# Row statistics of a tuned FNet/H3 kernel: eight rows' scaling, epsilon and bias moved from VectorE into ScalarE passes

## The chip, the core and the metric

The kernel runs on one core of a Trainium2 chip. A core has five engines, each with a queue of its own that it works off in order: TensorE (in the profile PE for matrix products and PEld for the loading of their weights), VectorE (DVE), ScalarE (ACT), GpSimd (POOL) and SyncE (SP), which here only issues transfers. An engine waits for another by a semaphore that stands on an instruction, and all that stands behind a waiting instruction waits with it. The metric is the device time of one execution in microseconds (us). Before the change it is 1183.71 us, the median of three runs (1183.38 to 1183.75).

## The reference, cut to what matters

```python
x = x + A(layernorm(x))      # layer 1
x = x + B(layernorm(x))      # layer 2
x = x + A(layernorm(x))      # layer 3
x = x + B(layernorm(x))      # layer 4

def layernorm(x):            # over the 576 channels of a row, eps = 1e-5
    return (x - mean(x)) / sqrt(var(x) + eps)

def A(x):                    # Fourier mixing, dft matrices given as arrays
    a = x @ dft_hid_re.T;  b = x @ dft_hid_im.T
    return dft_seq_re @ a - dft_seq_im @ b

def B(x):                    # gate: x times a long causal convolution
    kv = short_conv(k, shift_k) * v          # does not depend on x
    return x * (long_conv_fft(kv, ssm_k) + kv * ssm_D)
```

`x` is 2048 rows of 576 channels in float32. Only the normalisation of layer 1's input is touched by the change.

## The kernel before, in words

The 2048 sequence rows are cut into sixteen "rows" of 128 partitions by 576 channels; the text below calls them row 0 to row 15. Layer 1 multiplies them with the sequence matrix first. `layer` walks through 4 column blocks (`tb`) times 2 matrices (`g`, real and imaginary) times 16 rows (`k`), 128 steps in all. A step takes one 128x512 piece of the matrix (`c_mat`, loaded by SP, line 169) and one row of x. To keep float32 accuracy from products of a shorter float type, both are split into a high and a low part: ScalarE copies the high part (line 99 for the matrix, line 197 for a row of x), VectorE subtracts it from the source and keeps the low part (line 100 for the matrix, lines 204 and 205 for x). A step is 14 matmuls of 128x512: three (high by high, high by low, low by high) for each of four accumulators `s0` to `s3` and two for the remainder `rm`. The split pieces of the matrix lie in a ring of three, so a new one is written when the products of three steps before it are over.

The rows of x are needed one after the other in the first sixteen steps (`g` = 0, `tb` = 0). `get_x` is called three steps ahead (`XLEAD`): it asks for the row's load, takes its statistics (`stats0`) and normalises it in place, and `to_x` makes the two parts. Rows 0 to 7 have their statistics from VectorE (`normed`: bn_stats, bn_aggr, line 183 on). Rows 8 to 15 (`ASTAT` = 8) use `normed_x` with `sums`: ScalarE runs over the row with an accumulated sum (line 656), VectorE scales it to minus the mean (line 657), ScalarE runs again with that mean as bias, squares and accumulates (line 658), VectorE scales the sum and adds epsilon (line 659), GpSimd raises it to the power -0.5 (line 660), VectorE multiplies mean and factor to a bias (line 693), and ScalarE normalises (line 694). The three VectorE pieces are 128x1. Layers 2 to 4 use `sums` and `normed_x` too.

Beside these steps runs `branch`, the part of B that does not depend on x. In this stretch it makes the short convolution on VectorE (line 399 products, line 404 sums, both 128x1152; line 432 times v) and its first Fourier stage on TensorE: groups of six matmuls into the banks `bf` (`f1_products`), evicted by ScalarE into a staging tile `so` (line 458), which a transfer on ScalarE's queue stores to DRAM (line 459). There are four staging tiles, so an eviction waits until the store of four groups before it has landed. GpSimd's queue also loads the stage's matrices (line 173).

The program is written as one stream, and a scheduler with an own idea of the costs puts the instructions of each engine in an order; `behind` (`issue_after`) sets a few orders by hand. That order is fixed when the kernel runs.

## Time and profile before

| | before |
|---|---|
| median of three runs | 1183.71 us |
| the profiled execution: its time | 1181.68 us |
| its span, first to last instruction | 1179.9 us |
| TensorE busy | 1167.4 us, 99% of the span |
| VectorE busy | 869.3 us, 74% |
| ScalarE busy | 650.1 us, 55% |
| GpSimd busy | 76.3 us, 6% |

The profile is of one execution. Its page gives busy times by engine, and its views answer from the same trace: a timeline in order of time, groups of equal instructions, who waited for whom, and busy times in chosen windows. In a timeline row stand the start (us from the span's start), the duration, the engine, the source line, the operation, what it writes and reads, and how many equal ones follow each other; a bracket says how long the engine was idle before it and what ended that. The rows with "ACTq" or "SPq" are transfers being issued from an engine's queue. Matmuls overlap in the pipeline, so a run of twelve is read by the start of what follows it, not by the sum of the durations. Busy shares of the whole span are averages; the change touches only some 40 us of them near the start.

### The profile page before, as it was taken

Reading aid. Unit: us, or ns where it says so; the run is one execution under the profiler, and the core shown is the slowest. Engines: PE = TensorE matmul, PEld = TensorE weight load, DVE = VectorE, ACT = ScalarE, POOL = GpSimd, SP = SyncE. Lnnn points to the kernel's source line nnn. Section 1 sums busy time; section 2 is a strip of 40 time slices with the busy share of each in tenths; the row PEclk is TensorE's granted clock in tenths of the full one; section 3 lists DMA queues with packets and bytes.
Section 4 is the critical chain, followed back from the end, with each engine's and each line's share of the span. In section 5 each row is a group of like instructions: output and inputs, shape, how many; then the busy total and the mean of one; then the engine's idle time right before and its main releaser. Section 6 shows DMA issues by size and latency. Waiting matters only on the chain.

```text
span 1179.9 us, 18085 instructions
## 1 busy us (share of the span) xinstructions
PE 1167.4 (99%) x6198; PEld 988.8 (84%) x6198; DVE 869.3 (74%) x1564; ACT 650.1 (55%) x1280; POOL 76.3 (6%) x115
## 2 busy tenths in 40 slices
PE   8999999999999999999999999999999999999997
PEld 6776667988888888898888898888888888889997
DVE  7899983788877778777757765865776776775764
ACT  7865655577766667766645666534434445450200
POOL 2310000000000000001101111000000000001111
PEclk9999999999999999999999999999999999999999
DMA  9879898545666656648966777762862787895621
GB/s 337 284 230 308 267 293 289 164 151 171 211 215 196 203 168 202 182 149 245 269 187 221 244 251 226 256 237 76 257 247 72 223 291 251 262 329 152 222 89 41
DMA packets 147453, 255.64 MB, mean 217 GB/s; under 512 B 16161, under 2 KB 56353, under 8 KB 147362
## 3 DMA queue, kind: packets, MB, share of 16 engines
q1 hardware_dynamic: 111890, 210.17, 55.5%
q10 hardware_dynamic: 28560, 37.91, 9.1%
q0 software_dynamic: 6912, 6.43, 2.5%
q8 instruction: 48, 0.79, 0.3%
q14 instruction: 43, 0.35, 0.1%
HBM read 187.80 MB, written 66.65 MB: 216 GB/s over the span
## 4 chain that ended last, share of the span: by engine, by line
PE 86%; DVE 5%; DMA 4%; ACT 3%; issue 1%; SPq 0%; ACTq 0%; DVEq 0%
PE s L76 49%; PE bk L76 29%; PE rm L76 5%; PE bf L76 2%; DMA yb<-flts 2%; DMA flts<-in_c_mat 1%; ACT flts L519 1%; DVE f1f L404 1%; DVE f1f L399 1%; ACT mid L519 1%; DVE mats L100 1%; ACT mats L99 0%; DVE mid L525 0%; DVE f1r L100 0%; DMA ph<-in_c_mat 0%
## 5 line engine op out<-in xcount | busy, mean ns | idle before, releaser
L76 PE MATMUL s<-mats 128*128 128x512 f32 x2102 | 546.3, 395 | 4.2 <-DVE mats L766 1.5
L76 PEld LDWEIGHTS s<-mats 128*128 128x128 f32 x2102 | 382.4, 188 | 87.1 <-issue 10.8
L100 DVE TENSOR_TENSOR mats<-flts,mats 128x512 fp32r<-128x512 f32 x206 | 140.9, 688 | 51.6 <-ACT mats L99 49.7
L99 ACT ACTIVATE mats<-flts 128x512 fp32r<-128x512 f32 x206 | 128.2, 627 | 80.6 <-PE bk L76 31.1
L76 PE MATMUL bk<-mid 128*128 128x288 f32 x704 | 126.3, 300 | 0.8 <-ACT flts L519 0.2
L519 ACT ACTIVATE flts<-bk 128x288 f32<-128x288 f32 (+1 forms) x192 | 76.7, 406 | 90.8 <-PE bk L76 74.0
L76 PEld LDWEIGHTS bk<-mid 128*128 128x128 f32 x704 | 108.6, 188 | 21.2 <-ACT flts L519 4.8
L76 PE MATMUL bk<-w,u 128*128 128x288 f32 x864 | 120.3, 295 | 0.0
L76 PEld LDWEIGHTS bk<-w,u 128*128 128x128 f32 x864 | 117.4, 188 | 2.9 <-ACT flts L519 0.9
L525 DVE TENSOR_TENSOR mid<-flts,mid 128x576 fp32r<-128x576 f32 (+1 forms) x149 | 93.4, 627 | 18.9 <-ACT mid L519 16.0
L76 PE MATMUL rm<-mats 128*128 128x512 f32 x304 | 94.5, 390 | 0.2 <-ACT flts L519 0.2
L519 ACT ACTIVATE mid<-flts 128x576 fp32r<-128x576 f32 (+1 forms) x148 | 80.6, 576 | 9.1 <-DVE flts L540 5.1
L293 DVE TENSOR_TENSOR flts<-flts,bk 128x288 f32<-128x288 f32 x48 | 21.8, 454 | 68.6 <-PE bk L76 68.5
L76 PE MATMUL bk<-mats 128*128 128x288 f32 (+1 forms) x376 | 67.8, 317 | 0.0
L76 PEld LDWEIGHTS rm<-mats 128*128 128x128 f32 x304 | 56.9, 188 | 12.7 <-ACT flts L519 0.6
L458 ACT ACTIVATE flts<-bf 128x384 f32<-128x384 f32 (+1 forms) x104 | 43.3, 461 | 42.1 <-PE bf L76 39.8
L76 PE MATMUL s<-t,mats 128*128 128x512 f32 x264 | 64.9, 389 | 0.0
L186 POOL TENSOR_TENSOR flts<-flts 128x1 f32<-128x1 f32 x34 | 28.6, 843 | 515.6 <-DVE flts L185 514.1
L76 PE MATMUL bk<-mats,t 128*128 128x288 f32 (+1 forms) x368 | 59.3, 303 | 0.0
L519 ACT ACTIVATE flts<-flts 64x288 f32<-64x288 f32 x128 | 56.6, 443 | 4.5
L76 PEld LDWEIGHTS bk<-mats 128*128 128x128 f32 x376 | 55.6, 188 | 3.4
L76 PEld LDWEIGHTS s<-t,mats 128*128 128x128 f32 x264 | 49.5, 188 | 10.3
(152 smaller groups left out, 1495.9 us busy)
## 6 DMA issues: line engine op xcount, KB each, us to landing
flts<-in_c_mat SPq DMA_DIRECT2D x148, 256.0 KB, 3.5
ph<-in_c_mat SPq DMA_DIRECT2D x54, 512.0 KB, 4.2
flts<-in_c_mat SPq DMA_DIRECT2D x30, 512.0 KB, 5.2
flts<-td SPq DMA_DIRECT2D x53, 288.0 KB, 3.0
td<-flts ACTq DMA_DIRECT2D x36, 384.0 KB, 4.2
vd<-flts ACTq DMA_DIRECT2D x64, 144.0 KB, 2.4
flts<-vd SPq DMA_DIRECT2D x32, 288.0 KB, 4.1
ud<-ph ACTq DMA_DIRECT2D x12, 512.0 KB, 6.4
```

The lines of the kernel that those rows point to most:

```text
L76: return nc.tensor.matmul(ps, lhsT, rhs, start=first, stop=last, skip_group_check=more).ins
L99: a = nc.scalar.activation(h, src, AF.Copy).ins
L100: return a, nc.vector.tensor_tensor(l, src, h.bitcast(F32), OP.subtract).ins
L186: pows.append(nc.gpsimd.tensor_tensor(rs, ve, mhalf, OP.pow).ins)
L293: added[:] = [nc.vector.tensor_tensor(r[:, cs], r[:, cs], ps[:, :HD], OP.add).ins]
L399: nc.vector.tensor_tensor(out_t[:, n], k, wt[3 - t][:, n], OP.mult)
L404: nc.vector.tensor_tensor(rp, rp, out_t, OP.add)
L458: stored[:] = [nc.scalar.activation(so[:, i, :], ps[i], AF.Copy).ins]
L519: last_act.append(nc.scalar.activation(*args, **kw).ins)
L525: nc.vector.tensor_tensor(l, src, h.bitcast(F32), OP.subtract)
```

## The change

A new function `normed_first` serves rows 8 to 15 of layer 1 in place of `normed_x`. The scale by -1/576 goes into the first pass of ScalarE, so that its accumulated sum is minus the mean at once. The scale of the squares and the epsilon become a ScalarE instruction of 128x1 (Identity with scale 1/576 and bias epsilon), and the bias, mean times factor, becomes another one (Copy with the factor as scale). GpSimd's power stays. So for each row three VectorE instructions of 128x1 go and two ScalarE instructions of 128x1 come. `sums` and `normed_x` stay as they are for the later layers.

```diff
+    def normed_first(src, y, junk):
+        m = ring["stat"]()
+        sm, sv, rs, nb = (m[:, i:i + 1] for i in range(4))
+        nc.scalar.activation(junk, src, AF.Copy, scale=-1.0 / D, accum_out=sm)
+        nc.scalar.activation(junk, src, AF.Square, bias=sm, accum_out=sv)
+        nc.scalar.activation(sv, sv, AF.Identity, bias=eps, scale=1.0 / D)
+        pows.append(nc.gpsimd.tensor_tensor(rs, sv, mhalf, OP.pow).ins)
+        yield
+        nc.scalar.activation(nb, sm, AF.Copy, scale=rs)
+        nc.scalar.activation(y, src, AF.Identity, bias=nb, scale=rs)
+
 ...
-            LN[j] = src, normed_x(src, src, ring["junk"]()) if j >= ASTAT else normed(src, src)
+            LN[j] = src, normed_first(src, src, ring["junk"]()) if j >= ASTAT else normed(src, src)
```

In the changed file the new lines are 699 (sum), 700 (squares), 701 (epsilon), 702 (power), 704 (bias) and 705 (normalise); lines from 707 on are 11 higher than before. The scheduler has made another order of it. It differs from the old one from the statistics of row 8 on until the first Fourier stage has done its first twenty groups or so, about the first 150 us; behind that only buffer numbers differ.

First place: ScalarE, where rows 11 to 13 are handled. Before, with what each instruction waits for in brackets (the engines' semaphores; DMAHW is a transfer):

```order
L694 ACTIVATE early<-early,flts 128x576 [waits DVE_49]
L99 ACTIVATE f1r<-f1f 128x576 [waits DVE_49]
L197 ACTIVATE mats<-early 128x576 [waits Activation_49]
L99 ACTIVATE mats<-flts 128x512 [waits DMAHW4_49,PE_49]
L656 ACTIVATE early,flts<-early 128x576 [waits DMAHW0_49]
L459 DMA td<-flts 256x1x288
L459 DMA td<-flts 256x1x288 [waits DMAHW5_49]
L658 ACTIVATE early,flts<-early,flts 128x576 [waits DVE_49]
L694 ACTIVATE early<-early,flts 128x576 [waits DVE_49]
L658 ACTIVATE early,flts<-early,flts 128x576 [waits DVE_49]
L197 ACTIVATE mats<-early 128x576 [waits Activation_49]
```

The same place of ScalarE's queue in the change, from row 11's high part to row 12's:

```order
L197 ACTIVATE mats<-early 128x576 [waits Activation_49]
L99 ACTIVATE f1r<-f1f 128x576 [waits DVE_49]
L458 ACTIVATE flts<-bf_66 128x288 [waits DMAHW7_49,PE_49]
L458 ACTIVATE flts<-bf_67 128x288
L99 ACTIVATE mats<-flts 128x512 [waits DMAHW1_49]
L699 ACTIVATE early,flts<-early 128x576 [waits DMAHW6_49]
L704 ACTIVATE flts<-flts 128x1 [waits Pool_49]
L700 ACTIVATE early,flts<-early,flts 128x576 [waits Activation_49]
L705 ACTIVATE early<-early,flts 128x576 [waits Activation_49]
L701 ACTIVATE flts<-flts 128x1 [waits Activation_49]
L197 ACTIVATE mats<-early 128x576 [waits Activation_49]
```

No pass of the statistics waits for VectorE any more. Two rows are interleaved, so that hardly an instruction needs the one directly ahead of it, and what waits for GpSimd is now ScalarE (L704).

Second place: VectorE in the same stretch, where the low part of step 11's matrix piece (`mats<-flts,mats`) is made. Before:

```order
L432 TENSOR_TENSOR f1f<-f1f,flts 128x576 [waits DMAHW6_49,DVE_49]
L399 TENSOR_TENSOR f1f<-f1f 128x1152
L659 TENSOR_SCALAR flts<-flts 128x1 [waits Activation_49]
L399 TENSOR_TENSOR f1f<-f1f 128x1152
L204 TENSOR_TENSOR mats<-early,mats 128x64 [waits Activation_49]
L205 TENSOR_TENSOR mats<-early,mats 128x512
L100 TENSOR_TENSOR f1r<-f1f,f1r 128x576 [waits DVE_49]
L100 TENSOR_TENSOR mats<-flts,mats 128x512 [waits DMAHW2_49,PE_49]
L657 TENSOR_SCALAR flts<-flts 128x1
L693 TENSOR_TENSOR flts<-flts 128x1 [waits Pool_49]
L100 TENSOR_TENSOR mats<-flts,mats 128x512 [waits DMAHW4_49,PE_49,Activation_49]
```

In the change, the same piece of work:

```order
L404 TENSOR_TENSOR f1f<-f1f 128x1152 [waits DVE_49]
L100 TENSOR_TENSOR mats<-flts,mats 128x512 [waits DMAHW3_49,PE_49,Activation_49]
L432 TENSOR_TENSOR f1f<-f1f,flts 128x576 [waits DMAHW5_49,DVE_49]
L399 TENSOR_TENSOR f1f<-f1f 128x1152 x2
L204 TENSOR_TENSOR mats<-early,mats 128x64 [waits Activation_49]
L205 TENSOR_TENSOR mats<-early,mats 128x512
L100 TENSOR_TENSOR f1r<-f1f,f1r 128x576 [waits Activation_49]
L100 TENSOR_TENSOR mats<-flts,mats 128x512 [waits DMAHW1_49,PE_49,Activation_49]
```

The 128x1 instructions and their waits for GpSimd are gone, and the two-input instructions stand directly behind each other.

Third place: ScalarE near the last rows, with a store (L459) and the eviction that waits for its landing through the same staging tile (L458 with the same DMAHW name). Before:

```order
L459 DMA td<-flts 256x1x288 [waits DMAHW2_49]
L694 ACTIVATE early<-early,flts 128x576 [waits DVE_49,Activation_49]
L99 ACTIVATE f1r<-f1f 128x576
L197 ACTIVATE mats<-early 128x576 [waits Activation_49]
L458 ACTIVATE flts<-bf_66 128x288 [waits DMAHW5_49,PE_49]
L458 ACTIVATE flts<-bf_67 128x288
```

In the change:

```order
L459 DMA td<-flts 256x1x288 [waits DMAHW4_49]
L704 ACTIVATE flts<-flts 128x1 [waits Pool_49]
L700 ACTIVATE early,flts<-early,flts 128x576 [waits Activation_49]
L705 ACTIVATE early<-early,flts 128x576 [waits Activation_49]
L701 ACTIVATE flts<-flts 128x1 [waits Activation_49]
L197 ACTIVATE mats<-early 128x576 [waits Activation_49]
L458 ACTIVATE flts<-bf_68 128x288 [waits DMAHW4_49,PE_49]
```

Before, the DMAHW5 of the eviction was the store that stood some twenty-five instructions ahead; in the change the store that the eviction waits for stands five computing instructions ahead of it. On SP's queue one load of x has moved ahead of one load of the matrix at about 5.6 us.

## The prediction, as it was put on record

> **What bounds the kernel now.** I read the page first, then the windows of the first 140 us, TensorE's timeline there for its gaps, and at each gap the timeline of the engine that ended it. The page says who is the bound:
>
> ```profile
> PE 1167.4 (99%) x6198; PEld 988.8 (84%) x6198; DVE 869.3 (74%) x1564; ACT 650.1 (55%) x1280; POOL 76.3 (6%) x115
> ```
>
> TensorE is busy for all but 12.5 us of the 1179.9 us span, and the change takes no matmul away. Only gaps of TensorE can be won, and only where the new order differs, in the first 150 us or so. The windows where rows 8 to 15 are made, and one behind them (x is a count; the values are busy us of 10):
>
> ```profile
> 40.00:50.00 10.00, 10.00 (x51) 7.64 (x49) 9.62 (x16) 8.85 (x21) 5.80 (x2) 1.00 0.95 324
> 50.00:60.00 10.00, 9.16 (x42) 6.28 (x40) 7.93 (x20) 8.16 (x17) 1.10 (x2) 1.00 0.42 148
> 60.00:70.00 10.00, 10.00 (x51) 7.69 (x49) 9.56 (x17) 7.47 (x16) 2.05 (x3) 1.00 0.75 225
> 110.00:120.00 10.00, 10.00 (x50) 7.07 (x50) 10.00 (x12) 5.95 (x13) 0.53 (x1) 1.00 0.99 329
> ```
>
> The columns are TensorE, its weight loads, VectorE, ScalarE, GpSimd, the granted clock (1.00), and transfers. TensorE loses time in 50 to 60 us (9.16, 42 matmuls instead of 51). TensorE's timeline shows where, and one later gap:
>
> ```profile
> 42.87 3.05 PE L76 MATMUL s<-mats 128*128 128x512 f32 x12
> 45.75 0.62 PE L76 MATMUL rm<-mats 128*128 128x512 f32 x2
> ...
> 50.06 0.96 PE L76 MATMUL s<-mats 128*128 128x512 f32 x3
> 51.62 2.35 PE L76 MATMUL s<-mats 128*128 128x512 f32 x9 [0.60 <-DVE mats L100]
> 53.81 0.62 PE L76 MATMUL rm<-mats 128*128 128x512 f32 x2
> 54.67 1.91 PE L76 MATMUL s<-mats 128*128 128x512 f32 x6 [0.25 <-ACT mats L197]
> ...
> 119.04 1.66 PE L76 MATMUL s<-mats 128*128 128x512 f32 x6
> 121.03 0.79 PE L76 MATMUL bf<-f1r 64*128 64x384 f32 x6 [0.32 <-ACT flts L458]
> ```
>
> The ends of matmuls are modelled, so I price a gap by starts. Undisturbed, twelve matmuls behind a bf group take 45.75 - 42.87 = 2.88 us, 0.24 each. Step 11 starts at 50.06; its fourth matmul was due at 50.78 and comes at 51.62: 0.84 lost to a low part that VectorE made late. The two remainder matmuls at 53.81 need about 0.48, so step 12 was due at 54.29 and starts at 54.67: 0.38 lost to row 12's high part on ScalarE. Together 1.2 us. At 119.04 six matmuls need 1.44 and the group comes at 121.03: some 0.5 lost, while VectorE is 100% busy.
>
> Why both parts were late stands in ScalarE's timeline:
>
> ```profile
> 24.92 0.67 ACT L656 ACTIVATE early<-early 128x576 f32<-128x576 f32 x1
> ...
> 35.82 0.78 ACT L658 ACTIVATE early<-early,flts 128x576 f32<-128x576 f32 x1 [0.38 <-DVE flts L657]
> 36.50 0.19 ACT L658 ACTIVATION_READ_ACCUMULATOR early<-early,flts 128x1 f32 x1
> 36.59 0.85 ACT L694 ACTIVATE early<-early,flts 128x576 f32<-128x576 f32 x1
> 37.35 0.61 ACT L99 ACTIVATE mats<-flts 128x512 fp32r<-128x512 f32 x1
> ...
> 40.18 0.52 ACTq L459 DMA_DIRECT2D td<-flts  x1
> ...
> 40.66 0.68 ACT L197 ACTIVATE mats<-early 128x576 fp32r<-128x576 f32 x1
> 41.23 0.69 ACT L458 ACTIVATE flts<-bf 128x288 f32<-128x288 f32 x2
> 41.81 0.62 ACT L99 ACTIVATE mats<-flts 128x512 fp32r<-128x512 f32 x1
> ...
> 51.66 0.78 ACT L658 ACTIVATE early<-early,flts 128x576 f32<-128x576 f32 x1 [1.92 <-DVE flts L657]
> ...
> 53.95 0.67 ACT L197 ACTIVATE mats<-early 128x576 fp32r<-128x576 f32 x1
> ```
>
> ScalarE stood 1.92 us just before the second gap, for a 0.15 us VectorE instruction that was queued behind convolution work. The view of waits adds such pieces up for the first 100 us:
>
> ```profile
> DVE flts L693 <- POOL flts L660: 3.8, 7, 0.7
> ACT early L658 <- DVE flts L657: 3.8, 6, 1.9
> ...
> ACT early L694 <- DVE flts L693: 1.3, 2, 0.7
> ...
> DVE flts L659 <- ACT early L658: 0.9, 3, 0.5
> ```
>
> **The change part by part.** *Taken from VectorE:* eight each of L657, L659 and L693. They show 0.15 us but follow each other closer than that:
>
> ```profile
> 38.12 0.15 DVE L659 TENSOR_SCALAR flts<-flts 128x1 f32<-128x1 f32 x1
> 38.18 0.14 DVE L657 TENSOR_SCALAR flts<-flts 128x1 f32<-128x1 f32 x1
> ```
>
> So 24 x 0.06 to 0.07 = 1.6 us of queue, and the waits of 3.8 and 0.9 with them: 6.3 us that VectorE's queue gains over some 38 us, far over the 0.84 by which step 11's low part was late. This gap goes unless ScalarE is late.
>
> *Added to ScalarE:* two instructions of 128x1 for each of eight rows. Before has no such pair; the nearest are these:
>
> ```profile
> 2.04 0.20 ACT L177 ACTIVATE flts<-flts 128x1 f32<-128x1 f32 x1
> 1174.54 0.29 ACT L672 ACTIVATE flts<-flts 128x1 f32<-128x1 f32 x1 [50.95 <-DVE flts L670]
> ```
>
> 16 x 0.20 = 3.2 us to 16 x 0.29 = 4.6 us. I take 0.20, since neighbours overlap by 0.1 (L694 shows 0.85 and its successor starts 0.76 later), but keep 0.29. Against it stand the waits of 3.8 + 1.3 = 5.1 us that end. Whether row 12 is in time I add up along the new order, from the first pass of row 8 (24.92 before, and the queue ahead of it is unchanged) to row 12's L197. Start to start a squares pass with its read of the accumulator takes 0.77 (35.82 to 36.59), a normalising pass 0.76, L197 0.57 (40.66 to 41.23), an eviction 0.29 (two to 41.81); a matrix split is 0.62 less the overlap of 0.1, and a sum pass with its read 0.67 + 0.19 less twice 0.1. There stand 6 sum passes (4.0), 6 squares (4.6), 6 normalisings (4.6), 6 L197 (3.4), 8 evictions (2.3), 5 splits (2.6), one f1r copy (0.6) and 11 small ones (2.2 to 3.2): 24.3 to 25.3 us. L197 of row 12 would start at 49.2 to 50.2 instead of 53.95. It is due, with 0.84 no longer lost, at about 53.4: a lead of 3.2 to 4.2 us, and step 12's 0.38 goes too. The same sum to row 15 gives a lead of 2.5 to 3.3.
>
> *The new wait:* L704 on ScalarE waits for GpSimd's power, and behind it stand the next row's squares and a matrix split. The new order leaves 1.1 to 3.1 us of other passes, mostly 2.4, between L701 that starts a power and its L704. The power takes 0.55 when undisturbed, which that covers; the worst row is dearer:
>
> ```profile
> 41.88 4.20 POOL L660 TENSOR_TENSOR flts<-flts 128x1 f32<-128x1 f32 x1 [2.99 <-DVE flts L659]
> 52.79 0.55 POOL L660 TENSOR_TENSOR flts<-flts 128x1 f32<-128x1 f32 x1 [2.83 <-DVE flts L659]
> ```
>
> VectorE says why:
>
> ```profile
> 41.85 1.35 DVE L399 TENSOR_TENSOR f1f<-f1f 128x1152 f32<-128x1152 f32 x1
> 43.12 0.69 DVE L205 TENSOR_TENSOR mats<-early,mats 128x512 fp32r<-128x512 f32 x1
> 43.72 1.35 DVE L404 TENSOR_TENSOR f1f<-f1f 128x1152 f32<-128x1152 f32 x1
> 44.99 0.69 DVE L100 TENSOR_TENSOR mats<-flts,mats 128x512 fp32r<-128x512 f32 x1
> 45.59 0.15 DVE L657 TENSOR_SCALAR flts<-flts 128x1 f32<-128x1 f32 x1
> ```
>
> That power ended at 46.08, 0.4 after the last of four two-input instructions (44.99 + 0.69 = 45.68): it got in when the one-input L657 came. Until now one in eight was caught so long. One caught power costs ScalarE 4.2 - 2.4 = 1.8 us, within the lead; an undisturbed one nothing. I take one such row, so nothing on the path. The Trainium skill, "SBUF — State Buffer", "Who interferes with whom", says that a VectorE instruction with two SBUF inputs holds the port pair shared with GpSimd for the whole instruction, and that whoever starts first blocks the other. Its tie of the blocking to two inputs agrees with the rows; but read as first come, first served, a power would wait for one instruction alone, 1.35 + 0.4 = 1.8 us at most, under most of the cover of 2.4, and the slower rival below would have no chance. The row at 41.88 lost three handovers instead, so the measurement decides, and that rival keeps its chance.
>
> *Stores moved:* L459 now stands five computing instructions ahead of an eviction that waits for its landing, some 2.1 us. The view of that line, 20 to 75 us:
>
> ```profile
> DMA to landing us min/median/max: 2.9/4.1/8.1
> ```
>
> ScalarE's queue issues a store a few places early (at 40.18, before L197 and two evictions that stand ahead of it had started), some 2 us more. So a store costs nothing at the median and 4 us at 8.1, which the lead all but covers; I take nothing. SP's swap puts one matrix piece one issue later; its split is not the next thing ScalarE does, so nothing. GpSimd's own loads (L173) stand behind the powers in the same order as before, and wait for TensorE.
>
> *Later:* behind the rows VectorE is the tight queue (10.00 of 10 in the window of 110 to 120) and has the same work as before. With its 6.3 us it should start on it early enough not to take back TensorE's 1.2; of the 0.5 at 121.03 I count nothing, its other end being all of it.
>
> Sum: 0.84 + 0.38 = 1.2 us less, the other terms zero. The profiled execution (1181.68, the span and 1.8 around it) lies 2.03 under the median; taken off the median, 1183.71 - 1.2 = 1182.5.
>
> **The rivals.** *The gain is used up* (0.20): one or two powers or stores are caught late in the row sequence, where the lead is shortest (2.5), and TensorE waits about as long as it did: 1183.4 to 1184.3.
>
> *ScalarE becomes the bound* (0.26, slower): VectorE no longer pauses, so powers stay locked out; its only one-input instructions there are the ones removed. Each costs 1.8 us as above. With the lead of 3.5 plus the 1.2 won, it decides from the third caught row on; four caught rows give 7.2 - 3.5 = 3.7 lost against 1.2 before, 1183.7 + 2.5 = 1186.2. For it speaks that VectorE's new order has runs of six or more two-input instructions; against it, that VectorE waits for ScalarE's L197 in each row, and there GpSimd gets in.
>
> *The later gap goes as well* (part of the forecast's range): 1.2 + 0.5, 1182.0. That the change does not do what it says cannot be: the new order has no 128x1 VectorE instruction for these rows.
>
> **How the numbers follow.** The forecast, 1181.6 to 1183.3, has 0.50; a gain beyond it, from an order that fits better for a reason I don't see, 0.04. The low end is 1183.71 - 1.7 - 0.4 for what three runs vary (1183.38 to 1183.75); the high end, 1186.0, leaves out about half of the slower rival. 0.2% is 2.4 us, about what can be told from no change here; faster than 1181.3 gets 0.04, slower than 1186.1 0.13, and the rest, 0.83, lies within.
>
> **What would show it.** Right: no gap at steps 11 and 12; L197 of row 12 starting near 50; no waits of ScalarE on VectorE for statistics; L704 waiting under 2 us in all. Wrong: powers of 3 us and more in a row with ScalarE idle "<-POOL", evictions waiting for "DMA td" or a gap of TensorE behind L99 or L197 in steps 13 to 16.

## The result: the gaps of steps 11 and 12 are gone, and the kernel is 0.9 to 1.8 us slower

| | before | changed | ratio, 95% interval |
|---|---|---|---|
| first comparison, median of 22 runs each | 1183.5 us | 1185.32 us | 1.0016 [1.0010, 1.0022] |
| second, 12 runs beside 35 | 1182.71 us | 1183.59 us | 1.0007 [0.9997, 1.0017] |
| third, 11 runs beside 35 | 1184.0 us | 1185.04 us | 1.0007 [0.9999, 1.0016] |

The forecast was 1182.5 us, 1.2 us faster. All three comparisons point the other way, by 0.9 to 1.8 us, though the intervals of two of them just reach 1. Single executions of one kernel differ by more than that (the 22 of the changed kernel reach from 1183.53 to 1187.98, those of before from 1182.06 to 1185.44), so below a time is always a ratio to runs of the kernel before on the same chip, and a trace is one execution. The profiled one of the changed kernel took 1183.53 us, the shortest of its 22, with a span of 1181.6 us. Its page:

```profile
PE 1167.8 (99%) x6198; PEld 989.1 (84%) x6198; DVE 867.2 (73%) x1540; ACT 651.7 (55%) x1296; POOL 76.5 (6%) x115
```

The engines have the work that the forecast said: 24 instructions fewer on VectorE (DVE), 16 more on ScalarE (ACT), TensorE (PE) as before. The timeline of the changed kernel where the two gaps were, and behind it (start, duration, engine, line, what it does; in brackets the idle time ahead and who ended it):

```profile
42.85 0.52 ACTq L459 DMA_DIRECT2D td<-flts  x1
...
44.84 4.24 POOL L702 TENSOR_TENSOR flts<-flts 128x1 f32<-128x1 f32 x1 [2.99 <-ACT flts L701]
...
48.08 0.71 ACT L458 ACTIVATE flts<-bf 128x288 f32<-128x288 f32 x2 [2.23 <-DMA td<-flts]
...
49.87 0.29 ACT L704 ACTIVATE flts<-flts 128x1 f32<-128x1 f32 x1
...
50.05 0.77 ACT L700 ACTIVATE early<-early,flts 128x576 f32<-128x576 f32 x1
...
50.64 1.18 PE L76 MATMUL s<-mats 128*128 128x512 f32 x4
...
51.76 0.68 ACT L197 ACTIVATE mats<-early 128x576 fp32r<-128x576 f32 x1
...
51.89 1.98 PE L76 MATMUL s<-mats 128*128 128x512 f32 x8
...
52.47 0.23 DVE L204 TENSOR_TENSOR mats<-early,mats 128x64 fp32r<-128x64 f32 x1 [2.43 <-ACT mats L197]
...
53.93 2.88 PE L76 MATMUL s<-mats 128*128 128x512 f32 x12
...
62.27 0.66 PE L76 MATMUL bf<-f1r 64*128 64x288 f32 x6 [0.30 <-ACT flts L458]
...
66.56 0.68 DVE L100 TENSOR_TENSOR mats<-flts,mats 128x512 fp32r<-128x512 f32 x1
...
67.30 2.14 PE L76 MATMUL s<-mats 128*128 128x512 f32 x8 [0.52 <-DVE mats L100]
```

Steps 11 (50.64 on) and 12 (53.93) run without a gap, and step 12 starts 0.74 us earlier than the 54.67 of before. But three things are new. The eviction at 48.08 stood 2.23 us for the landing of the store issued at 42.85. VectorE stood 2.43 us at row 12's low part (L204) until ScalarE had made the high part. And TensorE now waits at 62.27 for an eviction and at 67.30, step 15, for the low part that VectorE starts at 66.56. Before, that low part was made in good time and TensorE came to the same products without a gap, at 67.33:

```profile
63.58 0.69 DVE L100 TENSOR_TENSOR mats<-flts,mats 128x512 fp32r<-128x512 f32 x1
...
67.33 1.98 PE L76 MATMUL s<-mats 128*128 128x512 f32 x8
```

So by step 15 this trace has lost again the 0.74 us that it was ahead at step 12. The view of waits for 30 to 72 us names the first two (engine, line, what it waited for: us in all, times, longest). Before:

```profile
ACT early L658 <- DVE flts L657: 3.6, 5, 1.9
DVE flts L693 <- POOL flts L660: 3.1, 6, 0.7
...
ACT early L694 <- DVE flts L693: 1.3, 2, 0.7
```

Changed:

```profile
ACT flts L458 <- DMA td<-flts: 5.1, 3, 2.2
DVE mats L204 <- ACT mats L197: 5.0, 3, 2.4
```

ScalarE's waits for VectorE and VectorE's for GpSimd went, as meant. ScalarE's wait for landings and VectorE's for ScalarE came: 10.1 us in place of 8.0.

A further loss may lie at the very start. SyncE issues a load of x ahead of a matrix piece now. Before, an early matrix piece and its products came like this:

```profile
5.58 0.33 SPq L169 DMA_DIRECT2D flts<-in_c_mat  x1
...
9.12 0.73 PE L76 MATMUL s<-mats 128*128 128x512 f32 x2 [0.48 <-DVE mats L100]
```

and in the changed kernel 0.4 us later at its issue and 0.59 at the matmul:

```profile
5.98 4.02 SPq L169 DMA_DIRECT2D flts<-in_c_mat  x2
...
9.71 0.73 PE L76 MATMUL s<-mats 128*128 128x512 f32 x2 [1.00 <-DVE mats L100]
```

Further on, near 95 us, an eviction is late again. In the kernel before, the load of ssm_k issued at 89.83 was waited for 2.56 us:

```profile
89.83 0.33 SPq L424 DMA_DIRECT2D flts<-in_ssm_k  x1
93.08 0.69 ACT L99 ACTIVATE f1r<-flts 128x576 fp32r<-128x576 f32 x1 [2.56 <-DMA flts<-in_ssm_k]
```

In the changed kernel a matrix load is issued beside it at 92.12, since the low part that frees its landing tile was made later; the wait is 4.01 us, and TensorE's group behind the next eviction comes late (that the matrix load slows the other is argued from the order, not measured apart):

```profile
89.48 0.33 SPq L424 DMA_DIRECT2D flts<-in_ssm_k  x1
91.39 0.68 DVE L100 TENSOR_TENSOR mats<-flts,mats 128x512 fp32r<-128x512 f32 x1
92.12 0.33 SPq L169 DMA_DIRECT2D flts<-in_c_mat  x1
...
94.18 0.69 ACT L99 ACTIVATE f1r<-flts 128x576 fp32r<-128x576 f32 x1 [4.01 <-DMA flts<-in_ssm_k]
...
95.68 0.79 PE L76 MATMUL bf<-f1r 64*128 64x384 f32 x6 [0.73 <-ACT flts L458]
```

To compare many traces I add up TensorE's gaps: for each matmul the distance to the next one's start, less what that distance is undisturbed (the median in the trace of before: 0.227 us for 512 columns, 0.132 for 288, 0.172 taken for 384, half of it where a group uses 64 rows). The sums are good to about 0.2 us. By matmul number, in us; the names are those of the experiments below, and a number in brackets counts the traces:

| kernel (traces) | 1 to 40, up to 13 us | 41 to 200 | 201 to 250, 47 to 59 us, steps 11 to 13 | 251 to 300, to 70 us, steps 14, 15 | 301 to 330 | 401 to 450, near 95 us | ratio to before |
|---|---|---|---|---|---|---|---|
| before (2) | 4.7, 4.9 | 2.2 | 2.5, 2.7 | 0.5 | 0.7 | 1.3, 1.6 | 1 |
| changed (3) | 5.2, 6.7, 5.3 | 2.2 | 0.8 | 1.8, 1.1, 2.0 | 0.9 | 2.5, 3.3, 1.9 | 1.0016, 1.0007, 1.0007 |
| e2 loads put back | 5.1 | 2.2 | 2.5 | 2.3 | 0.9 | 2.7 | 1.0006 |
| n2 e2, no powers | 5.6 | 2.2 | 2.2 | 2.4 | 0.9 | 2.8 | 1.0013 |
| w1 e2, low parts 20, 21 | 4.8 | 2.2 | 2.3 | 2.5 | 0.9 | 1.3 | 1.0008 |
| e1 early stores (2) | 4.8, 5.3 | 2.3 | 1.3, 2.3 | 2.3 | 0.9 | 3.0, 3.5 | 1.0016, 1.0013 |
| n1 e1, no powers | 5.2 | 2.3 | 1.0 | 2.3 | 0.9 | 1.8 | 1.0002 |
| u1 e1, low parts 15, 20, 21 | 4.9 | 2.3 | 1.4 | 1.3 | 1.9 | 1.3 | 1.0008 |
| z1 e1, low part 15 | 4.8 | 3.1 | 2.1 | 1.3 | 1.9 | 2.3 | 1.0015 |
| z2 z1, no powers | 4.8 | 3.2 | 1.0 | 1.3 | 1.9 | 2.2 | 1.0005 |
| y1 z1, wait filled (2) | 4.6, 4.3 | 2.3 | 2.4 | 0.6 | 1.1, 1.2 | 2.5, 2.7 | 1.0004, 1.0003 |
| c1 y1, convolution freed | 5.0 | 2.3 | 5.6 | 0.5 | 0.7 | 1.4 | 1.0022 |
| c2 changed, convolution freed | 5.1 | 2.2 | 0.8 | 2.3 | 0.7 | 2.0 | 1.0003 |
| p2 scale alone | 5.1 | 2.3 | 4.5 | 0.5 | 0.7 | 1.4 | 1.0027 |
| b1 before, low parts 15, 20, 21 late | 4.9 | 2.6 | 3.1 | 0.6 | 0.8 | 2.4 | 0.9999 |

The changed kernel's means against those of before: +0.9 at the start (+0.5 without its second trace), -1.8 at steps 11 to 13, +1.1 at steps 14 and 15, +0.2 behind them, +1.1 near 95 us, of which 0.3 comes back by the 600th matmul (4.5 us of gaps from 451 to 600, against 4.8). That is +1.2 us, inside the 0.9 to 1.8 that the runs give. The stretches left out (331 to 400, and all behind 600) differ as much between the two traces of before as between the kernels; with 331 to 400 in it the sum would be about 0.7, so the table says where time went and came, and not how much to 0.5 us.

### The profile page after: what moved, and what is told of

Same layout as the page of the kernel before. It is cut to its first block, busy times and chain, and to the rows that moved or that the text cites. A ratio compares the mean times of both kernels' runs of the same rounds, so it can differ in the third digit from the quotient of the medians.

```text
span 1181.6 us, 18077 instructions
## 1 busy us (share of the span) xinstructions
PE 1167.8 (99%) x6198; PEld 989.1 (84%) x6198; DVE 867.2 (73%) x1540; ACT 651.7 (55%) x1296; POOL 76.5 (6%) x115
## 4 chain that ended last, share of the span: by engine, by line
PE 84%; DMA 6%; ACT 5%; DVE 4%; issue 1%; SPq 0%; ACTq 0%; DVEq 0%; POOL 0%
PE s L76 48%; PE bk L76 29%; PE rm L76 5%; PE bf L76 2%; DMA yb<-flts 1%; DMA early<-in_x 1%; ACT flts L519 1%; DMA td<-flts 1%; ACT mats L99 1%; ACT mid L519 1%; DMA flts<-in_c_mat 1%; DVE mats L100 1%; DVE mid L525 1%; DVE f1f L399 0%; DMA flts<-in_ssm_k 0%
## 5 line engine op out<-in xcount | busy, mean ns | idle before, releaser
L458 ACT ACTIVATE flts<-bf 128x384 f32<-128x384 f32 (+1 forms) x104 | 43.0, 462 | 48.4 <-PE bf L76 43.2
```

The costliest lines, as they stand in the source:

```text
L458: stored[:] = [nc.scalar.activation(so[:, i, :], ps[i], AF.Copy).ins]
```

## The experiments

**Is it real, and where: the same two kernels again.**

> The changed kernel again, beside the edits that undo its parts. If its loss is real, the median is 1 to 2 us above the kernel before (the 1.0016 of the first comparison is 1.9 us), and the profile has the same three places against the kernel before: TensorE 0.5 to 0.6 us later by 13 us (the x load ahead of the matrix piece), 1.7 us gained at steps 11 and 12, and about 1.3 us lost at steps 14 and 15, where evictions (L458) stand at "DMA td<-flts" for 2 us. If the loss is only scatter from run to run, the median is within 0.5 us of the kernel before and one or more of the three places is missing.

> The changed kernel a third time, for the mean and for another profile. Single executions of every kernel here differ by 2 us and more, and one trace shows one of them. If the swapped loads of SyncE cost time, TensorE's gaps up to the fortieth matmul add up to 5.2 us or more again, against 4.7 to 5.1 in the six traces of kernels that have the old order of the loads. If the late stores (L459) make the scatter, the wait of the eviction near 48 us for the landing of the store of 43 us is again 2 us or more, and stretches 10 to 14 are slower the longer it is.

> The kernel before once more, for a second profile of it. It tells which parts of the difference between the two traces are scatter of single executions. If the 0.5 us at 13 us and the 0.9 us near 450 us belong to the change, this trace agrees with the first one of before within 0.3 us at both places; if they are scatter of loads, it differs from it by as much as the changed kernel does. At steps 11 and 12 the gaps of 0.84 and 0.38 us, which hang on the order alone, should stand again within 0.2 us.

The times are in the first table; the kernel before against itself gave 0.9995 [0.9985, 1.0005]. More gaps at the start, the gain, and the losses at steps 14 and 15 and near 95 us stand in all three traces of the changed kernel. A difference of 1.0 us near 450 us in the first pair of traces fell: the second trace of before has it too (1.2 us more than its first there, and 0.9 more near 80 us). Nothing below rests on it.

**SyncE's swap undone (e2).**

```diff
-            nc.sync.dma_start(XL[j], x[:, j, :])
+            with behind(*anchor[-1:] if j == 4 else ()):
+                nc.sync.dma_start(XL[j], x[:, j, :])
```

> The changed kernel with one thing undone: SyncE issues the load of x for row 4 after the matrix piece again, as the kernel before does. All else keeps its order. Theory A (the swap of the two loads costs the 0.5 us seen by 13 us): TensorE's lag against the kernel before at 13 us falls from 0.5-0.6 us to under 0.2, row 1's statistics start near 7.3 us instead of 7.88, and the time is 0.5 us below the changed kernel's. Rival: the 0.5 us is scatter of the loads or is taken up by a later wait: the time is the changed kernel's within 0.2 us. Either way evictions keep standing at "DMA td<-flts" for about 2 us twice.

1.0006 [0.9998, 1.0015]: no difference from the changed kernel that the runs can tell. The start has 5.1 us of gaps in the trace, against 5.2 to 6.7, but that is no clear difference: all kernels with the old order of the loads have 4.3 to 5.6 there, those with the swap 5.1 to 6.7. So the swap's price is not shown. Steps 11 to 13 lost 1.7 us against the changed kernel, for the landing took longer:

```profile
43.41 0.52 ACTq L459 DMA_DIRECT2D td<-flts  x1
...
50.08 0.71 ACT L458 ACTIVATE flts<-bf 128x288 f32<-128x288 f32 x2 [3.67 <-DMA td<-flts]
...
50.55 0.66 PE L76 MATMUL bf<-f1r 64*128 64x288 f32 x6 [0.69 <-ACT flts L458]
```

6.7 us from issue to the eviction, against 5.2 in the changed kernel. Every trace of the changed kernel waited 1.9 to 2.5 us here, those of e2 and n2 (further down) 3.7 and 4.0. Why the same store lands later when one load, issued at about 5 us, is put back is open.

**Stores issued early (e1).** The next row's statistics are put behind the store, so that 14 to 48 computing instructions lie between a store and the eviction that waits for it. SyncE's two loads stand in the old order here too, as in e2.

```diff
-            nc.scalar.dma_start(t_d[:, j::J, to:to + n], so)
+            sent[:] = [nc.scalar.dma_start(t_d[:, j::J, to:to + n], so).ins]
 ...
-                with behind(*stored):
+                with behind(*stored, *(sent if j + 1 >= ASTAT else ())):
```

> The changed kernel with each store (L459) of the rows' stretch issued ahead of the next row's statistics passes, so that 14 to 48 computing instructions of ScalarE lie between a store and the eviction that waits for its landing, instead of 1 to 10; the two loads of SyncE stand in the old order here too. Theory B (late stores are what takes the gain back): no eviction waits for "DMA td<-flts" over 0.5 us before 75 us, the 1.3 us at steps 14 and 15 are not lost, and with the 0.5 us of the loads the time is 1.8 us below the changed kernel's, about 1183.4 us or less, up to 1.2 us under the kernel before. Rival C (ScalarE itself, with its added passes, is late for steps 13 to 16): evictions still come late there, now behind ScalarE's own passes with no DMA named, and the time is that of the kernel with only the loads put back. Rival D (POOL's powers are locked out and ScalarE waits for them): rows of ScalarE waiting for POOL of 1 us or more appear, and the time does not fall.

> The early stores again. With them the eviction near 47 us does not wait, and ScalarE arrives earlier at the bias (L704) of row 12: it then stands there for GpSimd's power (1.5 us in the first trace, the power took 4.5 us). If the power takes the place of the landing as the wait (rival D, in the place where the store stood before), this wait of 1 us or more stands here again, and the median stays above the kernel before by 1 to 2 us as in the first measurement (ratio 1.0016). If the first measurement was scatter, the ratio is within 1.0007.

1.0016 [1.0008, 1.0025] and 1.0013 [1.0004, 1.0022]. No eviction waits for a landing any more, and the time did not fall; e2, which has the same loads and the late stores and was run beside the first of these, stands at 1.0006, so that early stores made it some 1.2 us slower. Theory B failed as the whole explanation, and rival D came in, in the place where the landing had stood:

```profile
45.83 4.48 POOL L702 TENSOR_TENSOR flts<-flts 128x1 f32<-128x1 f32 x1 [3.34 <-ACT flts L701]
...
50.34 0.30 ACT L704 ACTIVATE flts<-flts 128x1 f32<-128x1 f32 x1 [1.54 <-POOL flts L702]
...
67.72 2.12 PE L76 MATMUL s<-mats 128*128 128x512 f32 x8 [0.76 <-DVE mats L100]
```

This power takes 4.24 us in all three traces of the changed kernel and 4.48 in both of this one. In the changed kernel ScalarE stands for the landing at the same time, so the power shows nowhere. In e1's first trace step 12 has no gap all the same. In its second the wait is 1.55 us again, and step 12 pays:

```profile
51.93 0.29 ACT L704 ACTIVATE flts<-flts 128x1 f32<-128x1 f32 x1 [1.55 <-POOL flts L702]
...
55.08 3.05 PE L76 MATMUL s<-mats 128*128 128x512 f32 x12 [0.95 <-ACT mats L99]
```

**The powers left out, with early stores (n1) and with late ones (n2).** The power of -0.5 of rows 8 to 15 is not taken, and the variance itself stands in as the factor, so the values are not those of the reference. No other instruction changes its place.

```diff
-        pows.append(nc.gpsimd.tensor_tensor(rs, sv, mhalf, OP.pow).ins)
+        rs = sv
```

> The early stores without GpSimd's powers of rows 8 to 15: the factor is the variance itself, so the power of -0.5 is left out for these rows; every other instruction of every engine keeps its place. Theory D2 (in the early-store kernel the caught power is what costs): ScalarE's wait of 1.5 us at L704 is gone, the gaps of TensorE behind ScalarE's matrix pieces at steps 12 to 15 shrink by 0.4 to 1 us, and the time is 0.5 to 1.5 us below the early-store kernel's. Theory C (ScalarE's own work is the limit there): TensorE's gaps at 61 us and 67 us stay and the time is the early-store kernel's within 0.4 us.

> The changed kernel with SyncE's loads in the old order, and the powers of rows 8 to 15 left out in the same way; stores stay late. Here the eviction near 48 us waits for the store's landing, and the power runs beside this wait. Theory B (the landing is the wait that counts): nothing changes, the time is within 0.4 us of the same kernel with the powers (ratio 1.0006 against the kernel before) and the waits at DMA td<-flts stay at 4 to 6 us in all. Theory D: the time falls by 0.5 us or more.

n1 1.0002 [0.9993, 1.0010], n2 1.0013 [1.0002, 1.0024]. With early stores leaving out the eight powers is worth 0.0011 to 0.0014, 1.3 to 1.7 us. The traces show part of it at the caught power: the gap of 0.95 us at step 12 of e1's second trace is gone, but its first had none there, and n1 is also lower near 95 us (1.8 us of gaps against 3.0 and 3.5). With late stores leaving it out gains nothing, since the landing is then the longer wait (3.98 us in this trace). The two waits lie side by side: whoever removes one meets the other.

**Step 15's low part (z1, z2), and the wait filled (y1).** With both waits gone n1 stands at 1.0002, not 1.2 us below. Its gap at step 15 is left (2.3 us in the table). z1 holds one convolution pass back, so that VectorE makes this low part first, as before; z2 is z1 without powers; y1 is z1 with row 12's bias and normalising pass behind row 13's squares.

```diff
-                    for _ in range(-(-left // (2 * (later[0] - n) - half)) if left > 0 else 0):
+                    for _ in range(min({15: 12}.get(len(anchor), J * 7) - made_ops, -(-left // (2 * (later[0] - n) - half)) if left > 0 else 0)):
 ...  (y1)
-        nc.scalar.activation(sv, sv, AF.Identity, bias=eps, scale=1.0 / D)
+        squared[:] = [nc.scalar.activation(sv, sv, AF.Identity, bias=eps, scale=1.0 / D).ins]
 ...
-            with behind(*rounded[-1:]):
+            with behind(*rounded[-1:], *(squared if j in (12,) else ())):
```

> The early-store kernel with one convolution pass held back, so that the low part of step 15's matrix piece is made ahead of it as in the kernel before; two or three instructions change places on each engine. Theory E15 (this low part is most of the loss at step 15): the gap of 0.7 us behind L100 at 67 to 68 us is gone, the gaps between the 250th and the 300th matmul shrink from 2.3 us by 0.7 to 1.2 us, and the time falls by as much against the early-store kernel (1.0016 and 1.0013 against the kernel before), to 1.0004 to 1.0009. The wait of 1.5 us for the power stays. Rival C (ScalarE is late there anyway): the gap is taken over by ScalarE's matrix or eviction passes and the time stays within 0.4 us.

> The same with the powers of rows 8 to 15 left out (the factor is the variance itself). Now the landing, the power and the low part are all off TensorE's path. If the gain of the change was given back through these three alone, this kernel is under the kernel before by most of the forecast 1.2 us: ratio 0.9988 to 0.9996. If ScalarE's added instructions cost by themselves, it stays within 0.3 us of the kernel without powers (1.0002).

> The early stores and the old place of step 15's low part with all powers; row 12's bias and normalising pass stand behind row 13's squares, so that ScalarE works while GpSimd's power is caught. If the caught power is what is left, ScalarE's wait at L704 (here one line further down) falls from 1.5 us to under 0.3 us, and the time is 0.7 to 1.5 us below the same kernel without this, near or under the kernel before (0.9993 to 1.0003). If the two rows of delay push row 12's high part past its need, a gap of 0.3 us or more stands behind ScalarE's high part at step 12 and the time does not fall.

> The kernel with early stores, step 15's low part and the filled wait once more. If the first measurement holds, the ratio to the kernel before is 1.0000 to 1.0008, under the 1.0015 of the kernel without the fill, and ScalarE has no wait over 0.3 us for GpSimd.

z1 1.0015 [1.0006, 1.0024]: the gap at step 15 is gone (steps 14 and 15 go from 2.3 to 1.3 us), and 1.0 us more is lost right behind, at step 16, in the column 301 to 330. E15 failed: the gap moves, it doesn't go. z2 1.0005 [0.9996, 1.0014], 1.2 us under z1, and the table has 1.1 us less at steps 11 to 13: the second pair for the powers. It was expected under the kernel before if the landing, the power and the low part were all that gave the gain back; it is not, and lies some 0.4 us from the kernel without powers (1.0002), near what was expected if ScalarE's added instructions cost by themselves. Its trace shows where the gap went:

```profile
71.44 2.80 PE L76 MATMUL s<-mats 128*128 128x512 f32 x11 [1.15 <-DVE u L100]
```

y1 1.0004 [0.9995, 1.0013] and 1.0003 [0.9994, 1.0012]: with the powers in, the time is that of z2, 1.3 to 1.4 us under z1, and ScalarE no longer waits for GpSimd (the power is caught for 5.09 us). This is no third pair for the power, though. The edit changes the order on ScalarE and VectorE and moves a group of six matmuls on TensorE, and y1 is better elsewhere: 1.4 to 1.6 us less at steps 14 to 16 and 0.8 less in the column 41 to 200, where z1 and z2 have two gaps at 21 us. At steps 11 to 13 it has 0.3 us more. The gap at step 12 stands behind row 12's high part, as in the kernel before (lines are one higher here, L198 is L197):

```profile
54.74 1.67 PE L77 MATMUL s<-mats 128*128 128x512 f32 x6 [1.22 <-ACT mats L198]
```

**Convolution passes freed (c1 on y1, c2 on the changed kernel).** The passes of the short convolution are ordered by hand behind the low part of the row two steps ahead, so they wait with it when ScalarE is late.

```diff
-            with behind(made[min(n + 2, J - 1)], *evac):
+            with behind(made[min(n + (1 if n > 7 else 2), J - 1)], *evac):
```

> The kernel with early stores, step 15's low part and the filled wait, in which from step 8 on the convolution passes stand behind the low part of the row one step ahead instead of two. Theory V (VectorE's new wait for ScalarE's high part is what takes the rest): VectorE's waits at the low part (one line further down here) fall from 5.3 us to under 2.5 us between 30 and 72 us, and the time is 0.5 to 1.5 us below the same kernel without this, that is under the kernel before (0.9988 to 0.9999). If VectorE's wait costs TensorE nothing, the time stays at 1.0004 within 0.4 us.

> The changed kernel with that one edit alone; swapped loads and late stores stay. Theory V expects less waiting of VectorE at L204 (5.0 to 6.5 us before) but the eviction waits for landings stay (4.4 to 5.3 us), so the time falls by 0 to 0.8 us at most against the changed kernel (1.0007 to 1.0016). If VectorE's wait is the chief cause, it falls by 1.2 us or more.

c2 1.0003 [0.9994, 1.0011], the lowest of the kernels with late stores. Its waits from 30 to 72 us:

```profile
ACT flts L458 <- DMA td<-flts: 3.4, 2, 2.0
DVE mats L100 <- ACT mats L99: 3.1, 2, 1.8
DVE mats L204 <- ACT mats L197: 2.1, 1, 2.1
```

VectorE's wait at L204 fell from 5.0 to 2.1 us, but its wait for ScalarE's high part of a matrix piece rose from 0.7 to 3.1:

```profile
DVE mats L100 <- ACT mats L99: 0.7, 1, 0.7
```

(this line is of the changed kernel). Together they went only from 5.7 to 5.2 us, so c2 hardly tests theory V. Landings are waited for less (3.4 us against 5.1), the power of this place is not caught at all (0.77 us), a gap of 1.19 us behind a low part came at 63.55, and the intervals of c2 and of the changed kernel overlap. Why c2 is low is not settled. c1 went the wrong way, 1.0022 [1.0014, 1.0031]. VectorE's waits at the low part did not shrink (5.5 us), and one power was caught for 7.50 us (7498 ns is the longest in the view of the line; the row of the timeline holds this power and the next, which took 0.54):

```profile
46.62 8.01 POOL L703 TENSOR_TENSOR flts<-flts 128x1 f32<-128x1 f32 x2 [3.47 <-ACT flts L702]
...
54.16 0.29 ACT L705 ACTIVATE flts<-flts 128x1 f32<-128x1 f32 x1 [2.03 <-POOL flts L703]
...
56.78 1.72 PE L77 MATMUL s<-mats 128*128 128x512 f32 x6 [2.97 <-ACT mats L198]
```

Step 12 waited longer than in any other kernel.

**One part of the change alone (p2).** The first pass gives minus the mean; the other two small steps stay on VectorE.

```diff
-        nc.scalar.activation(sv, sv, AF.Identity, bias=eps, scale=1.0 / D)
+        nc.vector.tensor_scalar(sv, sv, 1.0 / D, EPS, op0=OP.mult, op1=OP.add)
 ...
-        nc.scalar.activation(nb, sm, AF.Copy, scale=rs)
+        nc.vector.tensor_tensor(nb, sm, rs, OP.mult)
```

> One part of the change alone: the first pass gives minus the mean at once (the scale is in it), while scaling and epsilon of the variance and the bias stay in VectorE's small instructions. Stores of the rows stand partly as late as in the changed kernel (4, 15, 12, 1 and 10 computing instructions ahead of the evictions), and SyncE's two loads in the old order. Theory B expects one wait of about 2 us for "DMA td<-flts" where the store is one instruction ahead, and a time between the kernel before and the changed kernel, some 0.3 to 1.3 us above the kernel before, with a gap of 0.4 to 0.9 us back at step 11 or 12 where the statistics still pass through VectorE. If VectorE's part was never on the path, no gap comes back.

1.0027 [1.0018, 1.0036], more than expected and the slowest of all. It has the least of the change in it, the longest wait for a landing, and a larger gap back at step 11 than the 0.4 to 0.9 us expected:

```profile
47.56 0.71 ACT L458 ACTIVATE flts<-bf 128x288 f32<-128x288 f32 x2 [4.38 <-DMA td<-flts]
...
53.05 4.05 PE L76 MATMUL s<-mats 128*128 128x512 f32 x10 [1.54 <-DVE mats L100]
```

**VectorE's order alone (b1), and held back on the changed kernel (w1, u1).** b1 is the kernel before with the low parts of steps 15, 20 and 21 as late as the change has them. w1 is e2 with those of steps 20 and 21 early, u1 is e1 with all three early. The map is the same in both, but in w1 step 15's low part stays as late as in the change. In w1 and u1 one product with v is taken ahead of the last two passes of its convolution row.

```diff
 (b1, on before)
-        with behind(*stored):
+        with behind(*stored, *(conved[LATE[step]:][:1] if step in LATE else ())):
             halved[:] = split(t[0], t[1], raw)
 (w1, u1: as z1, with {15: 12, 20: 19, 21: 21, 27: 33})
```

> The kernel before, statistics untouched, with one thing of the changed kernel's order: VectorE makes the low parts (L100) of three matrix pieces, those of steps 15, 20 and 21, behind one to three more passes of the short convolution, exactly as far back as the changed kernel has them. Theory E (these late low parts are what the changed kernel loses at step 15 and near 95 us): TensorE gains a gap of 0.4 to 0.8 us at step 15 behind L100, the matrix loads behind them slip, the load of ssm_k at 89.8 us lands later and an eviction near 95 us comes about 1 us late; in all 1 to 2 us slower than the kernel before (ratio 1.001 to 1.0017). Rival: the order of VectorE is covered by TensorE's queue, nothing moves by more than 0.3 us, and the loss comes from ScalarE's added work.

> The changed kernel with the two loads of SyncE in the old order and the convolution passes held back so that the low parts of the matrix pieces of steps 20 and 21 are made as early on VectorE as in the kernel before; stores and step 15 stay as the change has them. Theory E: the 1.2 us lost near 95 us against the kernel before are gone, the 1.3 us at steps 14 and 15 stay, and the time is about 1 us below the same kernel without this edit, near the kernel before. Rival (ScalarE's added work or plain scatter): no change over 0.3 us near 95 us.

> The changed kernel with the early stores and, beside them, the low parts of the pieces of steps 15, 20 and 21 as early on VectorE as in the kernel before. If the gain of the change (1.2 to 1.7 us at steps 11 and 12) is given back only through the order in which the rest was put, all of it now shows: no gap behind L100 at step 15, no loss near 95 us, and a time 0.5 to 1.5 us below the kernel before (ratio 0.9987 to 0.9996), some 2 us below the same kernel with the early stores alone. If ScalarE's added passes are themselves a cost, TensorE still waits 0.5 us or more for ScalarE's matrix parts or evictions at steps 13 to 16, and the time is not under the kernel before.

b1 0.9999 [0.9990, 1.0008]. Theory E failed for step 15: the low part is made at 67.54 instead of 63.58, and TensorE does not notice, since it comes to it only at 68.50, 0.27 us after it is done (lines of b1):

```profile
67.54 0.69 DVE L100 TENSOR_TENSOR mats<-flts,mats 128x512 fp32r<-128x512 f32 x1
...
68.50 2.00 PE L76 MATMUL s<-mats 128*128 128x512 f32 x8
```

In the changed kernel TensorE reaches the same products at 66.78 (67.30 less the gap), and there the part is late. b1 comes late for another reason: its gaps at steps 11 to 13 are 0.4 to 0.6 us larger than in the kernel before. So it does not tell whether this low part alone would cost an otherwise unchanged kernel something. Near 95 us theory E holds in every trace: the kernels with the low parts of steps 20 and 21 early (before, w1, u1, c1, p2) have 1.3 to 1.6 us of gaps there, all others 1.8 to 3.5, b1 among them with 2.4 though nothing else of the change is in it. The step from 1.6 to 1.8 is narrow, and the times do not bear it out: b1 should be some 0.8 us slower and is not, w1 1.0008 [0.9999, 1.0016] is no better than e2, u1 1.0008 [1.0000, 1.0017] is 0.6 to 0.9 us under e1. It was expected under the kernel before if the order alone gave the gain back; it is not, and it still waits at steps 14 and 16 (0.39 us behind ScalarE's matrix part, 1.12 behind VectorE).

**What follows.** Shown in times, by two pairs that differ in nothing else (e1 and n1, z1 and z2): once no landing stands beside them, the powers of rows 8 to 15 cost 1.2 to 1.7 us (the intervals of each pair still overlap a little); one of the eight is caught and waited for, and only part of the sum is seen at its place. Shown in the traces, and not apart in time: late stores make ScalarE stand 3 to 7 us in all at evictions, and the landing hides the power; steps 14 and 15 lose 1.1 us in the changed kernel; with the low parts of steps 20 and 21 late, 1.1 us more is lost near 95 us. Not shown: that the swapped loads cost anything, and that the late stores are what made the changed kernel slower, for without them (e1) it is no faster. Argued only: that the 1.2 us of steps 11 and 12 cannot be won alone. Where the landing and the wait for the power are both out of the way (n1, z2, y1), a gap of 0.7 to 1.2 us still stands somewhere in steps 12 to 16, behind ScalarE in y1 and behind VectorE in n1 and z2, as if both queues set the pace there. The rival that ScalarE's sixteen added instructions cost time by themselves (about 2.9 us of its queue at 0.18 each) is left standing: z2 and u1 came out nearer to it than to the other expectation, and no run isolates it. None of the versions beats the kernel before. One with the filled wait of y1 and early low parts at steps 20 and 21, without the product that w1 and u1 take too early, was not tried.

## Why the prediction was wrong

The step that failed is the last one of the sum, "the other terms zero". The 1.2 us came and more, but what the new order moved beside the 128x1 instructions, priced at nothing term by term, gave it back: in the table 1.3 us at steps 14 to 16, 1.1 near 95 us and 0.5 to 0.9 at the start. Which moved instruction has which share stays open, as no single one put back brought the gain out. Term by term:

- *The gaps of steps 11 and 12 go, 1.2 us*: right, 1.7 to 1.9 us in three traces.
- *No waits of ScalarE on VectorE for statistics; small instructions at 0.20 us from start to start*: right. They show 0.28 to 0.30 us and take 0.18 (49.87 to 50.05).
- *Row 12's L197 at 49.2 to 50.2*: it came at 51.76, late by the 2.23 us of the landing, still in time for its step.
- *Stores moved, "I take nothing"*: wrong, and the first term to fail in the order of time; the prediction had named evictions waiting for "DMA td" as a sign against it. The reasoning had the price (up to 4 us) and set it against ScalarE's lead. The landing took 4.9 to 5.5 us from issue to the eviction at 48 us, which stood 1.9 to 2.5, and there the lead did cover it: TensorE has no gap. A second and a third wait of 0.7 to 0.8 and 1.7 to 2.1 us stood at 62 and 67 us. Behind the second TensorE lost some 0.5 us in two of the three traces; at 67 us its gap stands behind a low part of VectorE. The lead had been worked out for the high parts of x, and these evictions had none. In time the term is not shown as the cause: with the stores early the kernel is no faster.
- *The new wait, one caught power within the lead, "nothing on the path"*: the power was caught once, as foretold (4.24 us), and L704 did not wait. But it ran out beside the landing, and the lead was not put to the test: with the stores early L704 waits 1.5 us, and the powers cost 1.3 to 1.7 us. Of two terms priced at nothing one hid the other. On the rule of the Trainium skill weighed there ("SBUF — State Buffer", "Who interferes with whom"), first come, first served would have ended this power after one VectorE instruction; it took 4.24 us, while VectorE ran four more two-input instructions, so the measurement still decides.
- *Taken from VectorE, 6.3 us that its queue gains*: 4.9 to 6.5 us of it came back as waits at L204 for ScalarE's high part. The prediction names this wait, as something that lets GpSimd in, and gives it no price.
- *Later, VectorE starts early enough "not to take back TensorE's 1.2"*: wrong by 1.1 us near 95 us, in the traces. The work was the same; its order, low parts behind convolution passes, was not, and the place looked at (121 us) was not the one that moved.
- *SP's swap, nothing*: the start has 0.3 to 1.8 us more gaps than in the two traces of before, but other kernels with the old order have up to 5.6 us there, so this is not shown wrong.
- *The rivals*: "The gain is used up" is nearest in its time, 1183.4 to 1184.3 on a base of 1183.71; the measured rise of 0.9 to 1.8 us lies between it and "ScalarE becomes the bound". Four caught powers never came, and the one that was caught did not make the changed kernel slower.
- *The range* 1181.6 to 1186.0 holds 1185.32. That is no merit of the sum: three runs that differed by 0.4 us stood for a kernel whose runs differ by 3.4.

## What to carry to other kernels

When a change lets an in-order queue run earlier, price everything that the scheduler moved with it, not the instructions that the change names: here the gain was as foretold, and the traces lose it again in what was re-ordered around it. Two waits that stand side by side must be priced together; each alone looks free, and taking one away shows only the other. In the traces a change in the order of one queue shows up some 30 us behind the rows it was made for, through a tile that comes free later and a load that is then issued later: the comparison of orders has to be read to its end. And an edit that takes a wait away moves other instructions too, so a faster time is credited to the wait only where the trace is better at that place.

## What the runs showed of the hardware that I had not expected

A store of 288 KB issued at about 43 us landed 4.9 to 7.0 us later (the changed kernel three times, e2, n2), where the view of the line has a median of 3.9 us from 20 to 75 us in the changed kernel: the landing that an eviction hangs on is not priced by the median. What a caught GpSimd instruction of 128x1 takes is set by VectorE's order, to a hundredth: 4.20 us in both traces of the kernel before, 4.24 in all three of the changed one, 4.48 in both of e1, 5.09 in both of y1, 7.50 in c1, 0.77 in c2, against 0.55 undisturbed. So it is no bad luck of one execution, and can be moved or removed by the order alone. Two traces of one unchanged kernel differed by 2.8 us in TensorE's gaps, most of it in two lumps of about 1 us (near 80 and 450 us), so a lump in one pair of traces says nothing of a change until a second pair has it.
